# Attention feeding two expert stages: where the small constant of the softmax sums is added

## The chip, the cores and the metric

The kernel runs on one core of a Trainium2 chip. The metric is the device time of one execution in microseconds (us). TensorE is written PE in the rows (PEld is its weight load), VectorE is DVE, ScalarE is ACT, GpSimd is POOL and SyncE, which issues most of the transfers, is SP.

## The reference, cut to what matters

The program computes three things in a row, all in 32-bit floats: attention that keeps only the 32 largest scores of each row, a gated two-layer stage on all 2304 tokens, and a stage with eight experts of which each token uses its best two.

```python
# attention: 4 batches, 8 heads, 576 positions, width 64
scores = scale * np.matmul(q, k.transpose(0, 1, 3, 2))
kth = np.partition(scores, -32, axis=-1)[..., -32:-31]
scores = np.where(scores >= kth, scores, -1e9)
scores = scores - np.max(scores, axis=-1, keepdims=True)
attn = np.exp(scores)
attn = attn / (np.sum(attn, axis=-1, keepdims=True) + 1e-09)
x = np.matmul(attn, v)            # -> [2304, 512]
# gated stage
h = x @ w_in
x = (h * np.clip(h + 3.0, 0.0, 6.0) / 6.0) @ w_out
# eight experts, two for each token, weighted by a softmax over noisy logits
```

The change touches one thing: the `1e-09` in the divisor of the attention.

## The kernel before

The kernel has two parts. The first (`phase_a`, up to about 850 us) does the attention, and beside it the gated stage, and beside that, piece by piece, the logits and the routing of the experts. The second (`phase_b`) does the experts.

The attention works on 144 heads, called `i` below: 18 tiles of 128 rows with 8 heads each. A loop over steps `st` (line 584) runs them as a software pipeline. In one step, seven or more heads are in work, each at another stage: the transposed query of head `st` (`q_evac`), the scores of head `st-1` (`scores`, `s_evac`, which leave them in `ss`), the maxima of seven segments of head `st-1` (`seg`), the search in them for head `st-2` (`chain`, whose result is `a`), a mask `z` by `zmask` for head `st-2`, the product `y` of mask and scores by `ysum` and the exponential `e` by `expo` for head `st-3`, the search for the 32nd largest score in `y` (`ymax`, into `t`) and the masking of `e` with its row sum (`pmask`, into `sum`) for head `st-4`, then the transposes of `e` for head `st-5` (`ptrans`), and in every second step the product with V for a pair of heads (`av`). So a head pair takes two steps, and there are 72 pairs.

The row sums of a pair stand in one tile `sum` of 128 rows and 2 columns. In every second step three functions turn them into factors: `recip1` on GpSimd adds 1e-9 (line 413), `recip2` on VectorE takes the reciprocal (line 416), and `recip3` on GpSimd spreads it over 2x64 columns into `rb` (line 421), which TensorE transposes one step later.

Beside the attention, from step 25 on, each step does one unit `u` of the gated stage: 12 matmuls into `h` (`mm1`), a relu on ScalarE into `r` (`hrelu`), the gate on VectorE (`hgate`), a rounding on ScalarE into `g` (`hround`), the rest on GpSimd (`hlow`), and 6 matmuls into `xa` (`mm2`). There are 144 units, so they run on for about 15 steps after the attention.

Each engine runs its own instructions in order and waits only for semaphores. From step 22 on (`KEEP`) the order on the four computing engines is that in which the Python code issues the work; before that, and for what is filled in, a scheduler with a model of times decides it. Within a step the order on GpSimd is `hlow`, `ysum`, `recip1`, the small `nbias` (tile `a`), `recip3`, then the scaling of the attention's result (`xscale2` into `xs`, `xsplit` into `xT`), the splitting of queries and keys (`qsb`, `ksb`), and last what `fill` holds. On VectorE it is `ymax`, `recip2`, then `chain` and `seg` mixed, `hgate`, `zmask`, `pmask`, the last segments.

Three kinds of step carry more than this. Where a new batch begins, the keys of its eight heads are split and transposed too (`k_split`, `k_trans`). After each chunk of two tiles, TensorE does the logits of the experts (tiles `lt`, `lg`). After six tiles the routing of their tokens follows, with many small operations on GpSimd and VectorE and then twelve indirect transfers from GpSimd that scatter the token lists into `idw` (line 813), four in each of three consecutive head pairs.

The last two tiles are routed by VectorE while the expert stage has begun. Its matmuls are `hb` (first layer, line 935) and `ac` (second layer, line 959). The route's counting matmuls `po` (lines 784 to 789) stand among them in TensorE's order. Behind `po` come the last scatter into `idw`, the load of the token lists `id`, the gather of tokens `xg` (line 868), and the transposes `et` (line 899) of the next expert job.

Of the kernel before, what the change touches and what calls it, by code (L numbers as in the profile page):

```python
# [7 lines left out]
F32 = mybir.dt.float32  # L8
# [5 lines left out]
ALU = mybir.AluOpType  # L14
# [162 lines left out]
def phase_a(tc, pools, ident, q, k, v, w_in, w_out, X, worst, wscr, stream, begin, on_chunk=None, slots=NSLOT, pace=None):  # L177
    nc = Lanes(tc)
    wp, ap, mp, ps, dr = pools
    TS, TT, STT = nc.vector.tensor_scalar, nc.vector.tensor_tensor, nc.vector.scalar_tensor_tensor  # L180
# [57 lines left out]
    def k_load(i):  # L238
        dl, b, h = ksched[i]
        KR[i] = kr = ap.tile([128, 5, 64], F32, name=f"kr{i}", tag="kr", bufs=KRB)  # L240
        nc.sync.dma_start(kr[:, 0:4, :], k[b, h, 0:512, :].rearrange("(p j) d -> p j d", j=4))
        nc.sync.dma_start(kr[0:64, 4, :], k[b, h, 512:576, :])
# [53 lines left out]
    def q_load(t, g):  # L296
        QR[t, g] = qr = ap.tile([128, 4, 64], F32, name=f"qr{t}_{g}", tag="qr", bufs=QRB)
        for (b, row, n, s0) in pieces(t):
            nc.sync.dma_start(qr[row:row + n], q[b, 4 * g:4 * g + 4, s0:s0 + n, :].rearrange("h s d -> s h d"))
# [24 lines left out]
    def scores(i):  # L324
        t, h = divmod(i, 8)
        p = ps.tile([128, 2, 512], F32, name=f"s{i}", tag="s")
        qts = QT.pop(i)
        for half in range(2):
            n = 2 * len(qts)
            m = 0  # L330
            for qt, (b, _, _, _) in zip(qts, pieces(t)):
                for j in range(2):
                    nc.tensor.matmul(p[:, half, 0:288], qt[:, j, :],
                                     KT[b, h][:, half * 288:(half + 1) * 288],
                                     start=(m == 0), stop=(m == n - 1))
                    m += 1
        PSS[i] = p

    def s_evac(i):
        p = PSS.pop(i)  # L340
        ss = ap.tile([128, 576], F32, name=f"ss{i}", tag="ss", bufs=SSB)
        nc.scalar.copy(ss.rearrange("p (a n) -> p a n", a=2), p[:, :, 0:288])
        SS[i] = ss
        ST[i] = ap.tile([128, NSEG, 8], F32, name=f"seg{i}", tag="seg", bufs=SEGB)
# [23 lines left out]
    def expo(i):  # L368
        if i % 2 == 0:
            EP[i // 2] = ap.tile([128, 1152], F32, name=f"e{i}", tag="e", bufs=EB)  # L370
        e = EP[i // 2][:, 576 * (i % 2):576 * (i % 2) + 576]
        E[i] = e
        nc.scalar.activation(e, SS[i], AF.Exp, bias=A8[i][:, 24:25], scale=0.125)
# [7 lines left out]
    def ysum(i):  # L381

        Y[i] = y = ap.tile([128, 584], F32, name=f"y{i}", tag="y", bufs=YB)
        nc.gpsimd.tensor_tensor(y[:, 0:576], Z.pop(i), SS[i], op=ALU.mult)

        nc.scalar.activation(y[:, 576:584], rank, AF.Relu, bias=fillc, scale=low[:, i:i + 1])
# [17 lines left out]
    SUM = {}  # L404

    def pmask(i):
        if i % 2 == 0:
            SUM[i // 2] = ap.tile([128, 2], F32, name=f"sum{i}", tag="sum", bufs=3)
        STT(E[i], SS.pop(i), T8[i // 8][:, i % 8, 7:8], E[i], op0=ALU.is_ge, op1=ALU.mult,
            accum_out=SUM[i // 2][:, i % 2:i % 2 + 1])  # L410

    def recip1(p):
        nc.gpsimd.tensor_scalar(SUM[p], SUM[p], 1e-9, 1.0, op0=ALU.add, op1=ALU.mult)

    def recip2(p):
        nc.vector.reciprocal(SUM[p], SUM[p])

    def recip3(p):
        r = SUM.pop(p)
        rb = ap.tile([128, 2, 64], F32, name=f"rb{p}", tag="rb", bufs=2)  # L420
        nc.gpsimd.tensor_scalar(rb, r[:, :, None].to_broadcast([128, 2, 64]), 1.0, 1.0, op0=ALU.mult, op1=ALU.mult)
        RB[p] = rb
# [42 lines left out]
    def xscale(p):  # L465
        xs = ap.tile([128, 256], F32, name=f"xs{p}", tag="xs", bufs=XSB)
        copy('a', xs, AVP.pop(p)[:, 0:256])
        XR[p] = xs
# [23 lines left out]
    def w_fetch(u):  # L492
        c, fb = u
        if fb in stream:
            w = wp.tile([128, 2, 1024], F32R, name=f"ws{c}_{fb}", tag="ws", bufs=NSTR)
            nc.sync.dma_start(w.bitcast(F32), wscr[fb])
            W[u] = w
        else:
            W[u] = wres[fb]

    def mm1(u):
        c, fb = u
        n = 128 * len(chunks[c])
        w = W[u][:, :, 0:512].rearrange("p a (d f) -> p a d f", d=4)
        xt = XT[c]
        p = ps.tile([128, 512], F32, name=f"h{c}_{fb}", tag="h")
        m = 0
        for d in range(4):
            for a, b in ((0, 0), (0, 1), (1, 0)):
                o = nc.tensor.matmul(p[:, 0:n], w[:, a, d, :], xt[b][:, d, 0:n], start=(m == 0), stop=(m == 11))  # L510
                m += 1
        HP[u] = p
        lastmm[:] = [o]
# [14 lines left out]
    def hround(u):  # L528
        n = 128 * len(chunks[u[0]])
        g = mp.tile([128, 2, 256], F32R, name=f"g{u[0]}_{u[1]}", tag="g", bufs=GB)  # L530
        copy('g', g[:, 0, 0:n], R[u][:, 0:n])
        G[u] = g

    def hlow(u):
        n = 128 * len(chunks[u[0]])
        g = G[u]

        eng = nc.vector if ustep_of[u] > slots + OD else nc.gpsimd
        low = eng.tensor_tensor(g[:, 1, 0:n], R.pop(u)[:, 0:n], g.bitcast(F32)[:, 0, 0:n], op=ALU.subtract)
        if pace is not None:  # L540
            pace[:] = [low] if eng is nc.gpsimd else []
# [37 lines left out]
    ok = lambda i: 0 <= i < slots  # L579
# [4 lines left out]
    for st in range(-6, end):  # L584
        if st == -6: q_load(0, 0)
        if st == BEGIN: begin()
        if st == KEEP: nc.keep()
        if st % 4 == 0 and 0 < st // 4 + 1 < slots // 4: q_load(*divmod(st // 4 + 1, 2))
        for i, (dl, b, h) in enumerate(ksched):
            if max(dl - 4, min(i, 2) - 6) == st: k_load(i)  # L590
        for fb in wstep.get(st + 2, []): wk.load(fb)

        while fetched < len(units) and units[fetched][0] <= st + 3:
            w_fetch(units[fetched][1]); fetched += 1
        u, up = ustep.get(st), ustep.get(st - 1)
        s_, a, b, c, d, e, av_, x1, x2 = (st - x for x in (OS, OA, OB, OC, OD, OE, OV, OX, OY))
        ki = kdl.get(st)

        if up:
            hround(up)  # L600
            hlow(up)
        if ok(s_):
            scores(s_)
            s_evac(s_)
        if ok(c):
            ysum(c)
            expo(c)
        if ok(d - 1) and d % 2 == 0: recip1(d // 2 - 1)
        if u:
            mm1(u)  # L610
            hrelu(u)
        if ok(e):
            ptrans(e)
            ptevac(e)
        if ki is not None or ok(st):
            kq_trans(ki, st if ok(st) else None)
        if ok(st): q_evac(st)
        if ok(x1) and x1 % 2 == 0: xscale(x1 // 2)

        ch = chain(b) if ok(b) else []  # L620
        segs = [(a, j) for j in range(NSEG)] if ok(a) else []
        if ok(d): ymax(d)
        if ok(d - 1) and d % 2 == 0: recip2(d // 2 - 1)
        if ch:
            ch.pop(0)()
            nbias(b)
        while ch:
            if segs: seg(*segs.pop(0))
            ch.pop(0)()
        if segs: seg(*segs.pop(0))  # L630
        if u: hgate(u)
        if ok(b): zmask(b)
        if ok(d):
            pmask(d)
        while segs: seg(*segs.pop(0))

        if ok(d - 1) and d % 2 == 0: recip3(d // 2 - 1)
        if ok(x1) and x1 % 2 == 0: xscale2(x1 // 2)
        if up:
            mm2(up)  # L640
            if up[1] == NFB - 1: xout(up[0])
        if ki is not None:
            k_trans(ki)
            k_evac(ki)
        if ok(av_) and av_ % 2: av(av_ // 2)
        for i, (dl, b, h) in enumerate(ksched):
            if dl + VL == st: v_load(i)
        if ok(x2) and x2 % 2 == 0: xsplit(x2 // 2)
        if st % 4 == 2 and 0 <= st // 4 + 1 < slots // 4: q_split(*divmod(st // 4 + 1, 2))
        for i, (dl, b, h) in enumerate(ksched):  # L650
            if max(dl - 2, min(i, 2) - 5) == st: k_split(i)
        for fb in wstep.get(st, []): w_split(fb)
        for fb in wstep.get(st + 1, []): wk.convert(fb)
        room = NFILL if st < slots + OD else 3 * NFILL
        while fill and room > 0:
            room -= fill[0][0]
            fill.pop(0)[1]()
# [669 lines left out]
```

## Time and profile before

| | us |
|---|---|
| median of 3 runs | 1393.41 |
| lowest and highest of them | 1392.29, 1394.97 |
| the profiled execution's own time | 1381.3 |
| its span, first to last instruction | 1379.5 |
| mean granted TensorE clock, as a share of 2.4 GHz | 0.975 |

The rows come from one profiled execution. A row of the timeline gives the start, the duration, the engine, the operation, the tiles written and read, and in brackets the idle time of the engine before it with what ended it. The view of stretches gives, for a window in us, its length and then each engine's busy time with the number of instructions, then the granted TensorE clock, the share of busy transfer engines and GB/s. A TensorE that is busy is not at its peak: its matmuls overlap, and their ends are modelled.

### The profile page before, as it was taken

What the parts mean: (1) busy time and instruction counts of PE and PEld (TensorE: products, weight loads), DVE (VectorE), ACT (ScalarE), POOL (GpSimd) and SP (SyncE); (2) the same over time, 40 slices, a digit from 0 to 9 for tenths busy, and PEclk for the clock granted to TensorE, in tenths of its full rate; (3) what the DMA queues carried; (4) which work ended last, traced back from release to release, by engine and by line L of the source; (5) the groups of instructions that cost most, each with busy time, mean ns of one, the idle gap of its engine ahead of it and who ended that gap; (6) DMA issues with size and microseconds to landing.
All of it is one profiled execution on the core that took longest, in us unless ns stands there. A gap on an engine that the chain in (4) does not pass through costs nothing. (4 is left out here: it accounts for less than half of the span.)

```text
span 1379.5 us, 27084 instructions
## 1 busy us (share of the span) xinstructions
PE 1293.2 (94%) x9006; PEld 1121.2 (81%) x9006; DVE 948.3 (69%) x3560; ACT 770.2 (56%) x1709; POOL 829.9 (60%) x1159
## 2 busy tenths in 40 slices
PE   5878899999999989999999899899999999999996
PEld 3554689989888878898988688788988898898985
DVE  7999987899987978869989753446353545435241
ACT  6888777777778666777777554534322322222220
POOL 7666777677767786767687845133324547465451
PEclk9789999999999999999999999999999999999999
DMA  7776644545365353445544447846446556465431
GB/s 249 261 279 226 230 145 157 193 166 176 132 206 166 127 149 124 170 131 187 175 143 157 123 154 246 265 140 221 136 153 195 178 167 204 140 214 177 137 109 38
DMA packets 138100, 239.56 MB, mean 174 GB/s; under 512 B 39779, under 2 KB 93155, under 8 KB 123872
## 3 DMA queue, kind: packets, MB, share of 16 engines
q1 hardware_dynamic: 127600, 210.57, 46.1%
q0 software_dynamic: 10352, 27.18, 5.9%
q8 instruction: 73, 1.20, 0.4%
q14 instruction: 75, 0.61, 0.2%
HBM read 209.08 MB, written 31.64 MB: 174 GB/s over the span
## 5 line engine op out<-in xcount | busy, mean ns | idle before, releaser
L959 PE MATMUL ac<-w,hh 128*128 128x512 f32 x960 | 247.8, 400 | 1.6 <-ACT hh L941 1.5
L935 PE MATMUL hb<-xe,w 128*128 128x320 f32 (+2 forms) x1536 | 239.4, 311 | 1.0 <-DVE hh L942 0.5
L935 PEld LDWEIGHTS hb<-xe,w 128*128 128x128 f32 x1536 | 232.1, 189 | 10.0 <-issue 3.9
L87 DVE MAX8 seg<-ss 128x8 f32<-128x82 f32 (+1 forms) x1008 | 213.9, 231 | 4.1 <-ACT ss L87 3.7
L87 POOL TENSOR_TENSOR y<-z,ss 128x576 f32<-128x576 bf16 x144 | 205.3, 1426 | 11.7 <-DVE z L87 10.1
L941 ACT ACTIVATE hh<-hb 128x640 fp32r<-128x640 f32 (+2 forms) x72 | 46.6, 647 | 295.7 <-PE hb L935 295.7
L959 PEld LDWEIGHTS ac<-w,hh 128*128 128x128 f32 x960 | 172.8, 188 | 40.3 <-ACT hh L941 5.4
L942 DVE SCALAR_TENSOR_TENSOR hh<-hb,hh 128x640 fp32r<-128x640 f32 (+2 forms) x72 | 53.9, 749 | 213.2 <-ACT hh L941 213.2
L87 PE MATMUL h<-xT,ws 128*128 128x256 f32 x1188 | 159.1, 283 | 9.3 <-DVE r L87 7.9
L87 ACT COPY ss<-s 128x576 f32<-128x576 f32 x144 | 92.6, 643 | 134.6 <-DVE e L87 69.6
L87 PE MATMUL xa<-ws,g 128*128 128x512 f32 x594 | 163.9, 410 | 2.2 <-POOL g L87 0.9
L87 PEld LDWEIGHTS h<-xT,ws 128*128 128x128 f32 x1188 | 150.0, 190 | 12.8 <-DVE r L87 9.9
L921 POOL TENSOR_TENSOR w<-r,w 128x1024 fp32r<-128x1024 f32 x40 | 97.9, 2452 | 85.2 <-ACT w L919 73.4
L87 DVE SCALAR_TENSOR_TENSOR e<-ss,t,e 128x576 f32<-128x576 f32 x144 | 147.6, 1025 | 0.1
L87 POOL TENSOR_TENSOR g<-r,g 128x256 fp32r<-128x256 f32 x124 | 100.2, 808 | 39.8 <-issue 19.6
L87 PEld LDWEIGHTS xa<-ws,g 128*128 128x128 f32 x594 | 104.0, 190 | 23.6 <-POOL g L87 5.1
L87 DVE TENSOR_SCALAR_CACHE_REDUCE z<-ss,a 128x576 bf16<-128x576 f32 x144 | 115.8, 804 | 0.2
L87 ACT ACTIVATE e<-ss,a 128x576 f32<-128x576 f32 x144 | 110.6, 768 | 1.4 <-POOL a L87 1.4
L87 PE MATMUL s<-kt,qt 128*128 128x288 f32 x512 | 101.2, 321 | 7.8 <-ACT qt L87 6.8
L87 DVE MAX8 t<-y 128x8 f32<-128x584 f32 x144 | 107.8, 749 | 0.0
L975 POOL DMA_INDIRECT out_dram<-y,id x40 | 41.8, 1045 | 108.9 <-DVE y L974 86.7
L87 PE MATMUL pa<-ident,e 128*128 128x128 f32 x576 | 91.3, 283 | 15.4 <-DVE e L87 13.4
(427 smaller groups left out, 2617.2 us busy)
## 6 DMA issues: line engine op xcount, KB each, us to landing
ws<-wscr SPq DMA_DIRECT2D x99, 1024.0 KB, 4.8
r<-in_moe_w_dram SPq DMA_DIRECT2D x144, 256.0 KB, 3.1
wscr<-wsp SPq DMA_DIRECT2D x11, 1024.0 KB, 5.8
wraw<-in_moe_w_in_dram SPq DMA_DIRECT2D x16, 512.0 KB, 4.2
wraw<-in_moe_w_out_dram SPq DMA_DIRECT2D x16, 512.0 KB, 5.1
ck<-in_moe_w_in_dram SPq DMA_DIRECT2D x32, 256.0 KB, 3.4
ck<-in_moe_w_out_dram SPq DMA_DIRECT2D x32, 256.0 KB, 3.2
out_dram<-zero SPq DMA_DIRECT2D x18, 256.0 KB, 4.2
```

The lines of the kernel that those rows point to most:

```text
L87: o = f(*args, **kw)
L921: eng.tensor_tensor(w[:, 1], r, w.bitcast(F32)[:, 0], op=ALU.subtract)
L935: o = nc.tensor.matmul(p[:, half, 0:hn], w[:, a, d, :], XE[job][:, b, d, half * hn:(half + 1) * hn], start=(m == 0), stop=(m == 11))
L941: nc.scalar.activation(hv[:, 0], p[:, 0:nh, 0:hn], AF.Relu)
L942: LOW[:] = [STT(hv[:, 1], p[:, 0:nh, 0:hn], 0.0, h.bitcast(F32)[:, :, 0:n].rearrange("p a (b n) -> p a b n", b=nh)[:, 0], op0=ALU.max, op1 ...
L959: o = nc.tensor.matmul(ACC[job, j], h[:, a, j * 128:(j + 1) * 128], w[:, b, :], start=(x % NF2 == 0 and m == 0), stop=(x % NF2 == NF2 - 1 ...
L975: s = nc.gpsimd.indirect_dma_start(out=out, out_offset=bass.IndirectOffsetOnAxis(ap=t.bitcast(I32)[:, j, 1:2], axis=0), in_=y, in_offset=N ...
```

## The change

The addition of 1e-9 goes from GpSimd to VectorE. `recip1` and its call in the step are gone. `recip2` now has two instructions: a tensor_scalar with an accumulator output, which adds the constant to the two sums in place and writes the sum of the two results into a third column that nobody reads, and the reciprocal. The tile has a third column for it.

```diff
     def pmask(i):
         if i % 2 == 0:
-            SUM[i // 2] = ap.tile([128, 2], F32, name=f"sum{i}", tag="sum", bufs=3)
+            SUM[i // 2] = ap.tile([128, 3], F32, name=f"sum{i}", tag="sum", bufs=3)
...
-    def recip1(p):
-        nc.gpsimd.tensor_scalar(SUM[p], SUM[p], 1e-9, 1.0, op0=ALU.add, op1=ALU.mult)
-
     def recip2(p):
-        nc.vector.reciprocal(SUM[p], SUM[p])
+
+        TS(SUM[p][:, 0:2], SUM[p][:, 0:2], 1e-9, None, op0=ALU.add, op1=ALU.add, accum_out=SUM[p][:, 2:3])
+        nc.vector.reciprocal(SUM[p][:, 0:2], SUM[p][:, 0:2])
 
     def recip3(p):
-        r = SUM.pop(p)
+        r = SUM.pop(p)[:, 0:2]
...
-        if ok(d - 1) and d % 2 == 0: recip1(d // 2 - 1)
```

Lines below the edits stand two lower after it (935 becomes 933, 959 becomes 957).

VectorE's order at a head pair in the middle of the attention, before. The wait in brackets names the engine whose semaphore the instruction waits for; `t` is the result of `ymax`, `y` GpSimd's product, `ss` the scores.

```order
L87 SCALAR_TENSOR_TENSOR e_5563,sum_5695<-ss_5474,t_5177,e_5563 128x576
L87 MAX seg_5724<-ss_5722 128x8 x2
L87 MAX t_5852<-y_5725 128x8 [waits Pool_49]
L87 RECIPROCAL sum_5695<-sum_5695 128x2 [waits Pool_49]
L87 MAX a_5851<-seg_5724 128x8 [waits DVE_49]
L87 MAX seg_5812<-ss_5810 128x8 [waits Activation_49]
```

The same place after the change:

```order
L87 SCALAR_TENSOR_TENSOR e_5563,sum_5695<-ss_5474,t_5176,e_5563 128x576
L87 MAX seg_5724<-ss_5722 128x8 x2
L87 MAX t_5851<-y_5725 128x8 [waits Pool_49]
L87 TENSOR_SCALAR sum_5695<-sum_5695 128x2 [waits DVE_49]
L87 RECIPROCAL sum_5695<-sum_5695 128x2 [waits DVE_49]
L87 MAX a_5850<-seg_5724 128x8
```

The reciprocal no longer waits for GpSimd. It and the new instruction wait for VectorE's own semaphore instead.

The scheduler also places some other work anew: in the first 22 steps much of VectorE's order is changed, and later a few rows move. One such place lies at the start of the expert stage. TensorE's order there, before (`po` are the counting matmuls of the last routing, `hb` and `ac` the expert's two layers):

```order
L935 MATMUL hb_13958<-xe_13882,w_1_13892 128x384 x12
L959 MATMUL ac_0_13974<-w_0_13886,hh_13935 128x512
L959 MATMUL ac_1_13978<-w_0_13886,hh_13935 128x512
L959 MATMUL ac_2_13982<-w_0_13886,hh_13935 128x512
L784 LDWEIGHTS tri
L784 MATMUL po_13837<-oh_13774,tri 128x16
```

And after the change:

```order
L957 MATMUL ac_0_13974<-w_0_13886,hh_13935 128x512
L957 MATMUL ac_1_13978<-w_0_13886,hh_13935 128x512
L957 MATMUL ac_2_13982<-w_0_13886,hh_13935 128x512
L957 MATMUL ac_0_13974<-w_1_13892,hh_13971 128x512 x2
L957 MATMUL ac_1_13978<-w_1_13892,hh_13971 128x512 x2
L957 MATMUL ac_2_13982<-w_1_13892,hh_13971 128x512 x2
L933 MATMUL hb_13992<-xe_13882,w_2_13898 128x384 x12
L957 MATMUL ac_0_13974<-w_1_13892,hh_13971 128x512
L957 MATMUL ac_1_13978<-w_1_13892,hh_13971 128x512
L957 MATMUL ac_2_13982<-w_1_13892,hh_13971 128x512
L782 LDWEIGHTS tri
L782 MATMUL po_13837<-oh_13774,tri 128x16
```

The counting matmuls now stand behind 21 more matmuls: 6 of `ac`, 12 of `hb` and 3 of `ac`.

## Rows read from the trace of the kernel before

**Rows 1.** The page: span, then busy time, share and instructions of each engine.
```profile
span 1379.5 us, 27084 instructions
PE 1293.2 (94%) x9006; PEld 1121.2 (81%) x9006; DVE 948.3 (69%) x3560; ACT 770.2 (56%) x1709; POOL 829.9 (60%) x1159
```

**Rows 2.** Waits of VectorE, 0 to 814 us: total, times, longest.
```profile
DVE sum L87 <- POOL sum L87: 90.8, 62, 4.8
DVE seg L87 <- ACT ss L87: 3.7, 10, 0.6
```

**Rows 3.** Timeline, an ordinary head pair, 367 to 378 us.
```profile
367.94 0.17 DVE L87 RECIPROCAL sum<-sum 128x2 f32<-128x2 f32 x1 [0.48 <-POOL sum L87]
377.70 0.17 DVE L87 RECIPROCAL sum<-sum 128x2 f32<-128x2 f32 x1 [0.49 <-POOL sum L87]
```

**Rows 4.** Stretches: the start, where the first eight pairs run.
```profile
27.00:136.80 109.80, 84.17 (x431) 54.46 (x431) 108.65 (x395) 90.60 (x177) 73.54 (x90) 0.84 0.72 254
```

**Rows 5.** Stretches, 12 ordinary pairs: 269.3 to 337.7 and 638.0 to 687.1, sum.
```profile
sum 117.50, PE 117.50 PEld 105.28 DVE 109.16 ACT 87.90 POOL 83.92; mean PE 58.75 PEld 52.64 DVE 54.58 ACT 43.95 POOL 41.96
```

**Rows 6.** Stretches, the other 25 ordinary pairs in seven windows, sum.
```profile
sum 250.80, PE 244.81 PEld 219.45 DVE 223.18 ACT 174.49 POOL 173.76; mean PE 34.97 PEld 31.35 DVE 31.88 ACT 24.93 POOL 24.82
```

**Rows 7.** Stretches, 12 pairs with new keys, in three windows, sum.
```profile
sum 143.50, PE 140.65 PEld 126.20 DVE 106.17 ACT 115.84 POOL 101.23; mean PE 46.88 PEld 42.07 DVE 35.39 ACT 38.61 POOL 33.74
```

**Rows 8.** Stretches, six pairs with scatters, in two windows, and their sum.
```profile
488.40:527.20 38.80, 34.66 (x251) 30.12 (x249) 28.27 (x125) 24.50 (x62) 32.20 (x44) 0.91 0.46 134
749.90:787.90 38.00, 33.59 (x250) 29.14 (x248) 28.25 (x125) 24.01 (x61) 31.43 (x43) 0.96 0.44 130
sum 76.80, PE 68.24 PEld 59.27 DVE 56.51 ACT 48.51 POOL 63.63; mean PE 34.12 PEld 29.63 DVE 28.26 ACT 24.26 POOL 31.82
```

**Rows 9.** Timeline, a pair with scatters, 499 to 516 us.
```profile
501.89 0.17 DVE L87 RECIPROCAL sum<-sum 128x2 f32<-128x2 f32 x1 [4.79 <-POOL sum L87]
...
503.87 2.93 PE L87 MATMUL h<-xT,ws 128*128 128x256 f32 x12 [3.34 <-DVE r L87]
```

**Rows 10.** Stretches, nine pairs heavy on VectorE (136.8 to 181.6, 434.8 to 478.8), sum.
```profile
sum 88.80, PE 79.21 PEld 66.58 DVE 81.95 ACT 62.90 POOL 65.58; mean PE 39.60 PEld 33.29 DVE 40.98 ACT 31.45 POOL 32.79
```

**Rows 11.** Groups by line: busy us, mean ns of one, idle before it.
```profile
L87 DVE TENSOR_SCALAR_CACHE_REDUCE z<-ss,a 128x576 bf16<-128x576 f32 x144 | 115.8, 804 | 0.2
L87 DVE RECIPROCAL sum<-sum 128x2 f32<-128x2 f32 x72 | 11.8, 165 | 91.8 <-POOL sum L87 91.7
L87 DVE DVE_READ_ACCUMULATOR z<-ss,a 128x1 f32 x144 | 11.8, 82 | 0.0
```

**Rows 12.** Timeline of VectorE, two dependent small operations at 848.8 us.
```profile
848.79 0.19 DVE L771 TENSOR_REDUCE rs<-rt 128x4 f32<-128x32 f32 x1
849.01 0.19 DVE L772 TENSOR_TENSOR rt<-rt,rs 128x32 f32<-128x32 f32 x1
```

**Rows 13.** One tile, e on VectorE: duration minimum, median and maximum in ns.
```profile
L87 DVE SCALAR_TENSOR_TENSOR e<-ss,t,e x144: 789/862/2444, 27.1 to 812.5; 128x576 f32<-128x576 f32 x144
```

**Rows 14.** The chain that ended last, 886 to 925 us: start, us, what.
```profile
906.36 5.75 DMA idw<-pl,ix
...
914.57 5.03 DMA xg<-X,id
919.60 0.04 issue
919.64 0.66 PE et L899 x4
```

**Rows 15.** Timeline of TensorE, 862 to 925 us.
```profile
899.59 0.18 PE L784 MATMUL po<-oh,tri 128*128 128x16 bf16 x1
...
903.27 2.46 PE L959 MATMUL ac<-w,hh 128*128 128x512 f32 x9
...
919.64 0.66 PE L899 MATMUL et<-ident,xg 128*128 128x128 f32 x4 [2.41 <-DMA xg<-X,id]
```

## The prediction

> **What bounds the kernel now.** I read the page first. Over the whole span TensorE is busy 94% and VectorE 69% [rows 1], but that averages the attention with the expert stage, so I went on by stretches and looked at the waits of the engine that is changed.
>
> In the attention VectorE waits for almost nothing except GpSimd's addition: 90.8 us in 62 waits, the longest 4.8 us, against 3.7 us for the next kind [rows 2]. The reason is the order on GpSimd. The addition stands behind `ysum`, the product of 1.3 us or more, of the same step. VectorE needs that product only one step later, but through `recip1` it waits for it at once.
>
> Whether those 91 us set the time is another question, and the stretches answer it by kind of head pair. In each I ask what TensorE does while VectorE waits.
> - The first eight pairs, 27 to 136.8 us: VectorE is busy 108.65 of 109.80 us [rows 4]. It is the bound, and it does not wait for GpSimd's addition.
> - 12 ordinary pairs: TensorE is busy all 117.50 us, VectorE idle 8.3 us [rows 5]. A pair takes 9.8 us. The usual one has a wait of only 0.48 or 0.49 us [rows 3]. TensorE is the bound, as far as the rows tell.
> - 25 more ordinary pairs, some with logits: TensorE idle 6.0 of 250.80 us, VectorE idle 27.6 [rows 6]. Nearly the same.
> - 12 pairs with new keys: VectorE idle 37.3 us, but TensorE only 2.85 [rows 7]. The large waits here lie beside extra work of TensorE.
> - Six pairs with scatters: TensorE idle 8.6 us of 76.80, and its granted clock is 0.91 and 0.96 of 2.4 GHz [rows 8]. Here a wait of 4.79 us in front of the reciprocal makes the gate late, and TensorE then waits 3.34 us for the gate [rows 9].
> - Nine pairs heavy on VectorE (routing, and steps that lack units): TensorE idle 9.6 us, VectorE 6.85 [rows 10].
>
> So most of VectorE's wait lies beside a busy TensorE. Only the time in which TensorE is idle or slowed can come back.
>
> **The change, part by part.** It removes 72 additions and the waits for them, 91.7 us in front of the reciprocals over the whole kernel [rows 11].
>
> It adds two instructions to each pair on VectorE, the addition and the read of its accumulator, and a wait of the reciprocal for the addition's result. The trace has no such pair with two columns. From above it costs what the mask `z` with 576 columns does, 0.80 + 0.08 = 0.89 us; from below two reads of the accumulator, 0.16 us [rows 11]. The nearest row is a pair of dependent small operations, 0.22 us from start to start [rows 12]. With 0.08 for the read I take 0.30 us, 72 x 0.30 = 22 us for the whole kernel. In 62 pairs it stands where a wait for GpSimd goes [rows 2], mostly of 0.48 us or more, so it costs nothing there beyond making the gain smaller. In the first eight there is hardly such a wait and VectorE is the bound: 8 x 0.30 = 2.4 us, at least 1.3 and at most 7.
>
> The gain, by kind:
> - Scatter pairs: TensorE can win its 8.6 us idle and what the low clock took. 0.09 x 38.8 + 0.04 x 38.0 = 5.0 us at most. Together 13.6 us. GpSimd is late next: it is busy 63.63 of the 76.80 us [rows 8], which allows 13.2. It still waits now and then for ScalarE and VectorE, so I take 9.
> - Nine VectorE-heavy pairs: 6.85 us idle less 9 x 0.30 = 2.7 gives 4.
> - Pairs with new keys: TensorE's idle 2.85 us, so 3. VectorE then waits for ScalarE's relu in front of the gate.
> - 37 ordinary pairs: half of TensorE's 6.0 us, so 3.
> Sum of the attention: 19 us. Its bounds: nothing, and VectorE's whole wait less its new work, 91.7 - 22 = 70 us.
>
> GpSimd loses 72 small operations and spreads the sums right behind `nbias` as before. The spread needs the reciprocal, which now comes earlier. `sum` has three buffers as before, and the third column is read by nobody.
>
> **The scheduler's moves.** In the first 22 steps VectorE's order changes, but VectorE is busy 99% there [rows 4], so an order alone can win little. I count zero, with 4 us to either side.
> The move at the start of the expert stage is worth more. The last route's counting matmuls `po` began at 899.59 us. Now 6 `ac`, 12 `hb` and 3 `ac` stand ahead of them. In the trace that stretch ends behind the third of the nine `ac` that begin at 903.27 and take 2.46 with their overlap, at about 904.0 [rows 15]. So `po` comes 4.4 us later. What follows is the chain that ended last: scatter, token list, gather, and then the transposes `et` at 919.64 [rows 14], for which TensorE already waits 2.41 us [rows 15]. TensorE's order behind it is the same, so all of it is late: +4.4 us. Bounds: zero, if the scatter is held by something else, and 7, if TensorE's clock falls in the longer wait.
>
> **The sum.** -19 + 2.4 + 4.4 = -12 us against the profiled execution's own 1381.3 us: 1369. The median of the runs shown, 1393.41, is 0.9% above that execution, so I scale: 1393.41 x 1369.3 / 1381.3 = 1381.
>
> **Where the Trainium skill bears on it.** TensorE's busy time is 100% in the ordinary pairs, its weight loads 105.28 of 117.50 us, 90% [rows 5]. [...]
> The masking of `e` takes 789 ns at least, 862 in the median and up to 2444 [rows 13]. "GPSIMD Engine Reference", section "Key points", says that GpSimd shares its paths to SBUF with VectorE and that instructions with two SBUF inputs contend; the masking has two. By that rule time won could be lost again beside GpSimd, the second rival. The spread of the durations agrees with it.
>
> **The rivals.**
> 1. TensorE has room in the ordinary pairs, and VectorE's idle time is the limit there too. For it: VectorE is busy 93% in rows 5. Against it: TensorE's rows there leave no gap. VectorE is idle 8.3 + 27.6 = 35.9 us in the 37 pairs [rows 5, 6]; less 37 x 0.30 = 11 that is 25 instead of the 3 above, 22 us more: -34, or 1359.
> 2. VectorE and GpSimd collide. Without the wait GpSimd's products overlap more of VectorE's masking. If each of 144 maskings went 0.07 us above its present median [rows 13], VectorE would lose 10 us in all, and the whole would come to about -2: 1391, no change. For it: that spread. Against it: TensorE, not VectorE, is the bound in most pairs.
> 3. The other side: the delay of `po` decides. It costs 4.4 us and, if TensorE's clock falls in the longer wait, 7. If TensorE's order and ScalarE hold the attention so firmly that it wins under 5 us, the start's 2.4 us and this make it slower. With 2 us won and 7 lost: +7, 1401. For it: TensorE is idle under 3% of the time in the ordinary pairs and in those with new keys [rows 5 to 7], and the delay lies on the last chain [rows 14]. Against it: in the scatter pairs TensorE is seen to wait for the gate [rows 9].
> That the change does not do what it says I rule out by the order: the reciprocal no longer waits for GpSimd.
>
> **How the numbers follow.** The forecast, 1366 to 1390, has a chance of 0.66, rival 1 0.12, rival 2 0.12, rival 3 0.10. What a measurement of this kernel tells from no change is 0.2%, 2.8 us. Nearly all of the forecast and rival 1 and a sixth of rival 2 are faster by more: 0.79. Same: 0.11, slower: 0.10. The range goes from 1357, with rival 1 in it, to 1395, with rival 2 and the mild cases of rival 3; left out are a gain near the bound of 70 us and rival 3 at its full price.
>
> **What would show it.** Right: VectorE has no wait for GpSimd in front of the reciprocal; addition, read and reciprocal together take about 0.4 us; the ordinary pairs keep 9.6 to 9.8 us; the six scatter pairs come down from 76.8 to about 68 us with the clock near 1.00; the gap in front of `et` grows from 2.4 to about 6.8 us; VectorE's new waits are for ScalarE (`seg`, `r`). Wrong: ordinary pairs near 9.2 us (rival 1), maskings longer than 0.93 us in the median (rival 2), or an attention that ends less than 5 us earlier (rival 3). The weakest steps are TensorE's limit in the pairs with new keys and the nine VectorE-heavy pairs.

## The result, and the profile after

The changed kernel takes 1378.23 us (median of 4 runs, 1377.34 to 1383.01) against 1394.19 for the kernel before (median of 4): ratio 0.9892, 95% interval 0.9864 to 0.992. That is 16.0 us, where 12 were predicted (1381 of 1393). The two profiled spans are only 2.3 us apart, 1377.2 and 1379.5 [rows 1], because the profiled execution of the kernel before was 13 us shorter than its timed runs. Which chip these runs used is not on record; on two later chips, where both kernels ran side by side, the change won 8 and 9 us (below). So each mark is read in two or three profiles.

The page of the changed kernel, the span and the busy time of each engine:

```profile
span 1377.2 us, 27159 instructions
PE 1288.4 (94%) x9006; PEld 1116.6 (81%) x9006; DVE 948.5 (69%) x3704; ACT 769.2 (56%) x1709; POOL 812.8 (59%) x1087
```

VectorE has 144 instructions more and the same busy time as in [rows 1], GpSimd 72 fewer and 17 us less. The waits of VectorE up to 800 us (total, times, longest), and its groups on `sum` (busy us, mean ns of one, idle before):

```profile
DVE seg L87 <- ACT ss L87: 60.3, 64, 2.6
DVE r L87 <- ACT r L87: 6.9, 9, 1.4
...
DVE t L87 <- POOL y L87: 4.5, 4, 1.1
```

```profile
L87 DVE RECIPROCAL sum<-sum 128x2 f32<-128x2 f32 x72 | 11.8, 164 | 2.1
L87 DVE TENSOR_SCALAR_CACHE_REDUCE sum<-sum 128x2 f32<-128x2 f32 x72 | 9.6, 134 | 0.0
L87 DVE DVE_READ_ACCUMULATOR sum<-sum 128x1 f32 x72 | 5.7, 80 | 0.0
```

The wait of 90.8 us for GpSimd's sum [rows 2] is gone. Two thirds of it have come back one instruction later, as waits for ScalarE's `ss`, which themselves stand behind TensorE's scores. The timeline of VectorE in an ordinary pair shows the exchange:

```profile
366.75 0.75 DVE L87 MAX8 t<-y 128x8 f32<-128x584 f32 x1
367.42 0.13 DVE L87 TENSOR_SCALAR_CACHE_REDUCE sum<-sum 128x2 f32<-128x2 f32 x1
367.48 0.08 DVE L87 DVE_READ_ACCUMULATOR sum<-sum 128x1 f32 x1
367.59 0.17 DVE L87 RECIPROCAL sum<-sum 128x2 f32<-128x2 f32 x1
367.67 0.20 DVE L87 MAX8 a<-seg 128x8 f32<-128x56 f32 x1
368.16 0.25 DVE L87 MAX8 seg<-ss 128x8 f32<-128x82 f32 x1 [0.29 <-ACT ss L87]
```

From the addition's start to the reciprocal's it is 0.17 us here, 0.177 in the median of 72; the three together take 0.34, where about 0.4 was predicted.

**Where the time went.** The 72 reciprocals of the row sums mark the head pairs in every profile. The distance from one to another, in us, in two profiles of the kernel before and three of the changed one:

| from reciprocal to reciprocal | before | changed |
|---|---|---|
| 1 to 9, the start | 103.5, 106.2 | 104.7, 104.5, 107.3 |
| 9 to 13, VectorE-heavy | 37.0, 38.1 | 35.6, 36.5, 35.8 |
| 13 to 21, new keys and behind | 87.7, 87.7 | 86.9, 87.3, 86.9 |
| 21 to 33, ordinary | 118.2, 118.2 | 118.1, 118.1, 118.1 |
| 33 to 41, new keys, then routing | 91.4, 91.3 | 91.0, 91.0, 91.1 |
| 42 to 49, scatters and behind | 79.9, 79.9 | 73.4, 73.3, 73.4 |
| 49 to 55, new keys and behind | 69.7, 69.7 | 68.9, 68.9, 68.9 |
| 55 to 66, ordinary | 111.8, 111.8 | 111.9, 111.8, 111.9 |
| 66 to 72, scatters and behind | 64.3, 64.3 | 58.4, 58.3, 58.7 |
| 9 to 72, all of these | 669.6, 670.7 | 653.3, 654.4, 653.9 |

Outside the start the distances repeat within some tenths, on different chips. The attention gains 16 us, and 12 of them lie in the two stretches with scatters. TensorE's waits there, before (reciprocals 42 to 49, then 66 to 72) and after, show what went. `h` is the first matmul of the gated stage and `r` VectorE's gate:

```profile
PE h L87 <- DVE r L87: 5.7, 3, 3.3
PE h L87 <- DVE r L87: 5.9, 3, 2.7
```

```profile
PE xa L87 <- POOL g L87: 1.9, 2, 1.0
PE xa L87 <- POOL g L87: 2.5, 3, 1.0
```

The wait for the gate, 11.6 us, is gone, and what is left is mostly a wait for `g` from GpSimd. GpSimd's additions themselves took only 1.34 and 1.15 us in these two stretches before, so the work taken off GpSimd can't be the 12 us.

The view of stretches (length, busy time of PE, PEld, DVE, ACT and POOL with their instructions, granted clock, DMA share, GB/s) shows for the kernel before the scatter pairs with the pair behind them:

```profile
488.40:537.20 48.80, 42.70 (x309) 37.41 (x308) 37.79 (x166) 28.92 (x72) 39.54 (x55) 0.90 0.49 140
749.90:797.90 48.00, 41.31 (x316) 35.95 (x315) 37.76 (x166) 29.31 (x73) 38.11 (x53) 0.96 0.49 144
```

And for the changed kernel, first 12 ordinary pairs, then the same scatter pairs with the pair behind them:

```profile
268.60:386.70 118.10, 118.01 (x968) 106.18 (x967) 108.84 (x522) 86.02 (x215) 80.22 (x115) 1.00 0.48 159
486.90:530.60 43.70, 40.63 (x328) 35.41 (x326) 39.04 (x174) 30.36 (x75) 36.80 (x51) 1.00 0.61 164
741.10:783.70 42.60, 40.08 (x323) 34.82 (x322) 37.66 (x173) 29.80 (x74) 35.76 (x50) 1.00 0.57 163
```

The clock, 0.90 and 0.96 before, is 1.00 in both. TensorE is still idle for 5.6 us of them. In the ordinary pairs it stays busy all the time, and nothing is gained.

Behind the attention a part is given back. TensorE's row at the transposes of the next job, with the gap in front of it:

```profile
902.55 0.86 PE L957 MATMUL ac<-w,hh 128*128 128x512 f32 x3
910.05 1.12 PE L897 MATMUL et<-ident,xg 128*128 128x128 f32 x4 [6.63 <-DMA xg<-X,id]
910.82 2.91 PE L957 MATMUL ac<-w,hh 128*128 128x512 f32 x6
```

The gap was 2.41 us [rows 15]. In it the clock falls to 0.5, at 906.7 us, and stays there for 6.8 us: `et` takes 1.12 us instead of 0.66, and six `ac` take 2.91 where nine took 2.46. In the two later profiles of the changed kernel the gap was 4.95 and 6.51 us. From the last reciprocal to the 97th `hb`, behind all this, it is 123.1, 126.1 and 125.5 us, against 116.3 and 120.5 before.

### The profile page after: what moved, and what is told of

It is laid out like the page before. It is cut to its first block, busy times and chain, and to the rows that moved or that the text cites. A ratio compares the mean times of both kernels' runs of the same rounds, so it can differ in the third digit from the quotient of the medians.

```text
span 1377.2 us, 27159 instructions
## 1 busy us (share of the span) xinstructions
PE 1288.4 (94%) x9006; PEld 1116.6 (81%) x9006; DVE 948.5 (69%) x3704; ACT 769.2 (56%) x1709; POOL 812.8 (59%) x1087
## 4 chain that ended last, share of the span: by engine, by line
PE 64%; DVE 6%; issue 5%; ACT 4%; POOL 3%; DMA 1%; another core or an unknown queue 1%; POOLq 0%; ACTq 0%; SPq 0%
PE ac L957 15%; PE hb L933 15%; PE xa L87 10%; PE h L87 9%; PE av L87 5%; PE s L87 4%; PE pa L87 2%; DVE seg L87 2%; POOL idw L811 1%; DVE e L87 1%; PE et L897 1%; DVE z L87 1%; ACT ss L87 1%; DVE t L87 1%; PE lg L727 1%
## 5 line engine op out<-in xcount | busy, mean ns | idle before, releaser
L87 POOL TENSOR_TENSOR y<-z,ss 128x576 f32<-128x576 bf16 x144 | 201.2, 1397 | 14.7 <-DVE z L87 12.9
L87 DVE SCALAR_TENSOR_TENSOR e<-ss,t,e 128x576 f32<-128x576 f32 x144 | 143.6, 997 | 0.1
L87 POOL TENSOR_TENSOR xs<-xs 128x128 f32<-128x128 f32 x72 | 51.7, 718 | 119.4 <-ACT xs L87 119.3
L87 POOL TENSOR_TENSOR g<-r,g 128x256 fp32r<-128x256 f32 x124 | 96.4, 778 | 24.2 <-issue 9.2
```

Source lines behind the costliest of these rows:

```text
L87: o = f(*args, **kw)
```

## The experiments

My theory: VectorE stands behind GpSimd's `ysum` for nothing, but only where TensorE has room is the wait worth anything, and the late `po` gives some back. The rivals: VectorE is the limit nearly everywhere (rival 1 of the prediction), the new order of the start or of the scheduler makes the gain, or the form of the addition matters.

The runs used three more chips, on which the kernel before took 1398.12 us (the two kernels again, GpSimd ahead of `ysum`, `po` held ahead for the first time), 1384.95 us (the reciprocal later, four additions, no addition and the plain form for the first time) and 1385.00 us (the changed kernel for the third time, and every second measurement). So every time is compared by its ratio to the kernel before on its chip, and an expectation in us that was reckoned for another chip can't be held against the time; the marks in the traces can.

**The two kernels again, on another chip.** No edit.

> The kernel before, unchanged, for a second profile. Its first profiled execution took 1381.3 us, its timed runs 1394. Theory A: that execution was an unusually short one, and the extra 13 us lie in the attention (more stretches at half clock, or longer pairs): a second profile ends near 1394 and its last reciprocal of a row sum comes near 825 instead of 814 us. Theory B: they lie in the expert stage, behind 880 us: the last reciprocal stays at 814 and the time behind it grows by 13. If the profile again takes 1381, the profiled executions of this kernel are 13 us shorter than its timed ones for a reason that no row shows.

> The changed kernel, unchanged, for a second profile. Theory: 1378 us again; the attention ends (last reciprocal of a row sum) at 799 us, 13 to 15 before that of the kernel before. The new waits of TensorE behind the 13th et (for hh from ScalarE, some 6 us from there to the end in the first profile) come back if they follow from the change; if they were an accident of one execution they are gone and the profile ends near 1372.

Measured: 1399.33 us, and 1391.83 for the changed kernel, ratio to the kernel before 0.9941 (0.9908 to 0.9973). In the profile of the kernel before the last reciprocal came at 818.4 (3 of the 4 us from the start), and from the 97th `hb` to the end it took 464.6 us instead of 449.0: theory B for most of it. The changed kernel's last reciprocal came at 800.3, and TensorE's waits for `hh` came back, 8.9 us. The kernel before had 9.2 us of them here, so they belong to neither kernel alone. ScalarE pauses; its rows in the changed kernel:

```profile
1038.59 0.57 ACT L902 CAST xe<-et 128x512 fp32r<-128x512 f32 x1
1048.17 0.70 ACT L939 ACTIVATE hh<-hb 128x640 fp32r<-128x640 f32 x1 [9.01 <-issue]
```

Its input was complete 4.3 us before. In a third profile of the changed kernel (below) the same instruction started at once:

```profile
1041.76 0.58 ACT L902 CAST xe<-et 128x512 fp32r<-128x512 f32 x1
1047.09 0.71 ACT L939 ACTIVATE hh<-hb 128x640 fp32r<-128x640 f32 x1 [4.75 <-PE hb L933]
```

**GpSimd adds, ahead of `ysum`.** From the kernel before:

```diff
+        if ok(d - 1) and d % 2 == 0: recip1(d // 2 - 1)
         if ok(c):
             ysum(c)
             expo(c)
-        if ok(d - 1) and d % 2 == 0: recip1(d // 2 - 1)
```

> The kernel before with one line moved: GpSimd still adds the constant, but ahead of ysum instead of behind it. VectorE gets no new work, and the start and TensorE's order there stay as before; po comes late as in the changed kernel. My theory (the gain is the removed wait behind ysum, whoever adds): the wait in front of the reciprocal nearly goes, the last reciprocal comes 14 to 17 us earlier, the time is 1374 to 1381 us. Rival 1 (the gain comes from the new order of the first 22 steps or from taking work off GpSimd): no gain, 1392 to 1398. Rival 2 (GpSimd now waits at that addition for VectorE's masking, and ysum behind it is late): half the gain, 1383 to 1390, with new waits of GpSimd for sum.

Measured: 1393.81 us, ratio 0.9977 (0.9945 to 1.0009). From the 9th to the 72nd reciprocal it took 662.0 us, 8 less than before: half the gain. The time, with `po` late, is only 4.3 us under the 1398.12 of this chip. By the marks that is rival 2, with the waits that it named (VectorE, then GpSimd, 150 to 800 us):

```profile
DVE sum L87 <- POOL sum L87: 32.1, 23, 3.5
DVE sum L87 <- issue: 12.1, 4, 3.9
```

```profile
POOL sum L87 <- DVE e L87: 16.9, 22, 2.0
```

VectorE's and TensorE's order in the start is the old one here, so the new order of the start is not the source of this half.

**The reciprocal issued later.** From the kernel before; the call of `recip2` moves from in front of `chain` to behind it:

```diff
         if ok(d): ymax(d)
-        if ok(d - 1) and d % 2 == 0: recip2(d // 2 - 1)
...
+        if ok(d - 1) and d % 2 == 0: recip2(d // 2 - 1)
         if segs: seg(*segs.pop(0))
         if u: hgate(u)
```

> The kernel before with the reciprocal issued later in its step on VectorE, behind the search of chain and six of the segments, about 2 us on; GpSimd still adds, in its old place behind ysum. VectorE gets no new work and should find the sum ready. po comes late as in the changed kernel. My theory (the wait of VectorE is all that the change removes): the waits for sum fall from 91 us to under 20, the last reciprocal comes at 797 to 802 us instead of 814 to 818, 1386 to 1392 us on this chip. Rival (taking the addition off GpSimd matters as well, or the spread rb, which now comes later, holds up xs): the last reciprocal no earlier than 806.

Measured: 1383.48 us, ratio 0.9991 (0.9978 to 1.0003), and 663.0 us from the 9th to the 72nd reciprocal, 7 less than before. The last reciprocal at 808.1: the rival. VectorE's wait fell to 20.1 us, but GpSimd now waits for the reciprocal (waits of VectorE, then of GpSimd, 150 to 800 us):

```profile
DVE seg L87 <- ACT ss L87: 67.9, 68, 3.0
DVE sum L87 <- POOL sum L87: 20.1, 12, 5.7
```

```profile
POOL rb L87 <- DVE sum L87: 42.4, 40, 1.9
```

At the first scatters (reciprocals 42 to 49) it took 81.1 us, no less than before. There GpSimd itself is late, and only an addition that isn't behind its work helps: 73.4 in the changed kernel, 75.8 with GpSimd's addition ahead of `ysum`. My theory was too simple: it is not only VectorE's wait that costs, but the chain from GpSimd to VectorE and back to GpSimd. Each of the two runs eases one end of it and has about half the gain.

**Four additions instead of one, and none.** From the changed kernel:

```diff
-        TS(SUM[p][:, 0:2], SUM[p][:, 0:2], 1e-9, None, op0=ALU.add, op1=ALU.add, accum_out=SUM[p][:, 2:3])
+        (four times this line, with 5e-10; or no such line)
```

> The changed kernel with the addition and the read of its accumulator four times in a row instead of once (each adds 5e-10); po late as in the changed kernel. One addition with its read took 0.23 us from its start to that of the reciprocal, so VectorE gets 3 x 0.23 = 0.7 us more in each of 72 pairs, 50 us in all. My theory (outside the first eight pairs VectorE has room, since it now waits 61 us for ScalarE's scores): 5.5 us in the start, and of the other 44 us about a third, 12 to 25 us later in the last reciprocal. Rival 1 of the prediction (VectorE is the limit in the ordinary pairs): all of it, 45 to 50 us later. If VectorE has room everywhere but in the start: 5 us.

> The changed kernel without the addition: 1e-9 is left out. VectorE has 72 x 0.23 = 17 us less to do; po stands ahead of the ac of w_1 again, as in the kernel before, so the fair comparison is the changed kernel with po held first (1383 us on this chip). My theory (the added work costs something in the start and in the pairs heavy on VectorE alone): the start 1.8 us earlier, the last reciprocal 2 to 5 us earlier, 1378 to 1382 us. Rival 1 (VectorE is the limit nearly everywhere): the last reciprocal 12 to 17 us earlier, 1366 to 1371 us.

> The changed kernel without the addition (1e-9 left out), po ahead, beside the changed kernel with po held ahead. Theory (the added work on VectorE is nearly all hidden outside the start): within 2 us of that kernel, and 0 to 2 us under it. Rival 1 of the prediction (VectorE is the limit): 10 to 17 us under it.

Measured: with four 1388.21 us, ratio 1.0027 (1.0015 to 1.0039), which is slower than the kernel before. The last reciprocal came at 814.9, 12 to 15 us later than in the changed kernel, as the theory has it. From the 9th to the 72nd it took 665.2 us, 11 more than the changed kernel, where the new work is 38 us (0.77 us from the first addition to the reciprocal instead of 0.18, 63 times). The 12 ordinary pairs that took 118.10 us took 119.40:

```profile
275.00:394.40 119.40, 118.90 (x973) 106.59 (x973) 115.21 (x594) 87.32 (x217) 80.94 (x115) 1.00 0.47 161
```

VectorE's busy time grew by 6.4 us there and the stretch by 1.3, so VectorE isn't the limit; TensorE, busy 118.90 us, is the one left. In the 11 others (55th to 66th reciprocal) it was 115.5 us, 3.6 more for 6.5 of new work: there the room for more is small. Between the 9th and the 13th it was 38.8 us, 3 more for 2.4 of new work: VectorE is the limit there. The 5.5 us expected in the start did not appear there: the first reciprocal came 2 us later, at 43.5, and from it to the 9th took 106.1 us, inside the changed kernel's 104.5 to 107.3.

Without the addition: 1369.43 us, ratio 0.9882 (0.9864 to 0.99), and in the second measurement 1370.17, ratio 0.9899 (0.9883 to 0.9916), beside 1372.78 for the changed kernel with `po` ahead. From the 9th to the 72nd reciprocal it took 652.6 and 652.0 us, 1 to 2 less than with the addition. The last reciprocal, at 798.9 and 799.2, is less than 4 us earlier, not 12 to 17. Its start has an order of its own, and the stretch from the 42nd to the 49th is the same 73.3 and 73.4 us, so the order of the start doesn't make the gain. The first time lies in the bracket of rival 1, but that was reckoned for the chip where the kernel before took 1398. In the second measurement the difference of the medians is 2.6 us, a little over the 2 expected. So the 12.7 us that it adds on VectorE (72 x 0.177 from its start to the reciprocal's; the 0.23 of the expectations was too much) cost 1 to 2 in the path. Rival 1 is out for work of this size. In the reference the largest term of each row is exp(0) = 1, so the sum is at least 1, and 1e-9 lies far under the spacing of 32-bit floats there: leaving it out is, by the medians, the fastest version that was tried.

**`po` held ahead.** From the changed kernel, an order without a wait, as in the kernel before:

```diff
+            PO[:] = [o]                                 # o: the last counting matmul
...
+                    if g == 2: after(tc, o, PO[0])      # hb of w_2
...
+                    if g == 1: after(tc, o, PO[0])      # ac of w_1
```

> The changed kernel with the counting matmuls po held ahead of the ac of w_1 and the hb of w_2, as in the kernel before; everything else stands as in the changed kernel. My theory (the move of po gives back 4.4 us at the start of the expert stage): the gap in front of the 13th et falls from 6.6 to about 2.4 us, no stretch at half clock follows it, 1370 to 1375 us. Rival (the move is hidden, since the gather or ScalarE decides there): the same 1378 within 2 us.

> The changed kernel with po held ahead, as before, now compared with the changed kernel where it may be measured more closely. Theory (late po gives back 4.4 us and more, with half clock behind the gap): 4 to 8 us under the changed kernel. Rival (the 9 us seen so far were the other chip's pauses of ScalarE): within 2 us of it.

> The changed kernel, unchanged, as the reference for the three others on this chip. The last reciprocal at 799 to 801 us as in both profiles so far. From the 84th hb on, the time to the end was 455 us where ScalarE never paused and up to 16 us more where it did; if the pauses belong to the chip and not to the kernel, all four kernels here have them or none.

Measured: 1382.98 us, ratio 0.9899 (0.9869 to 0.993), where the changed kernel had 0.9941; then 1372.78, ratio 0.991 (0.9893 to 0.9928), beside 1375.57 for the changed kernel, 0.9936 (0.9921 to 0.9951). So 3 to 9 us by the medians, though the intervals overlap. The 2.8 us of the second measurement lie between the theory there (4 to 8) and its rival (within 2): part of the 9 us seen first were pauses of ScalarE, as the profiles say (from the 84th `hb` to the end 469.2 us, in the changed kernel there 475.3). By the medians it is under both kernels in both measurements. TensorE's rows in its second profile:

```profile
894.36 0.17 PE L785 MATMUL po<-oh,tri 128*128 128x16 bf16 x1 [2.44 <-DVE oh L777]
...
913.39 0.66 PE L901 MATMUL et<-ident,xg 128*128 128x128 f32 x4 [1.57 <-DMA xg<-X,id]
```

The gap in front of `et` is 1.57 us (none in the first profile), and the clock does not fall behind it. But TensorE now waits 2.44 us in front of `po` for VectorE's `oh`, which is last there: the routing allows little more. In this profile `po` came so late, 94.6 us behind the last reciprocal, that the way to the 97th `hb` took 124.5 us, as in the changed kernel; in the first it took 118.9.

**The plain form of the addition.** From the changed kernel; the order on every engine is the same:

```diff
-        TS(SUM[p][:, 0:2], SUM[p][:, 0:2], 1e-9, None, op0=ALU.add, op1=ALU.add, accum_out=SUM[p][:, 2:3])
+        TS(SUM[p][:, 0:2], SUM[p][:, 0:2], 1e-9, 1.0, op0=ALU.add, op1=ALU.mult)
```

> The changed kernel with the plain form of the addition, which has no accumulator to read; every engine's order stays that of the changed kernel. The read takes 0.08 us, 72 of them 5.8 us. My theory: 1 to 2 us earlier at the last reciprocal, no difference that the times can tell from the changed kernel's 1392 on this chip. If the plain form is slower by itself (another mode of the instruction), the pair from addition to reciprocal takes more than 0.23 us and the last reciprocal is not earlier.

> The changed kernel with the plain form of the addition, on the same chip as the changed kernel. In its first profile 72 plain additions took 33 us, 0.28 us in the median and up to 1.72, most of them ending 23 to 33 ns after a running product of GpSimd; with accumulator an addition took 0.13 us, 0.16 at most. Theory (the plain form is held until GpSimd's instruction ends, the form with accumulator is not): the last reciprocal 3 to 4 us later than in the changed kernel, the time 2 to 4 us longer. Rival (the 33 us lie beside a busy TensorE, and the later reciprocal was chance): within 1 us.

Measured: 1379.21 us, ratio 0.9954 (0.9938 to 0.9971); then 1380.04, ratio 0.9966 (0.9951 to 0.9981), against 1375.57 for the changed kernel on the same chip. The plain form is the slower one, by 4.5 us in the medians (the ends of the intervals meet) and with the last reciprocal 3.1 us later, though it has one instruction fewer. The tile on VectorE (duration minimum, median, maximum in ns), the plain form and then the changed kernel on that chip:

```profile
L87 DVE TENSOR_SCALAR sum<-sum x72: 142/280/1711, 41.3 to 805.1; 128x2 f32<-128x2 f32 x72
```

```profile
L87 DVE TENSOR_SCALAR_CACHE_REDUCE sum<-sum x72: 124/133/155, 41.1 to 802.4; 128x2 f32<-128x2 f32 x72
```

The timeline says why. First the plain form, beside GpSimd's product, then the form with accumulator at the same place:

```profile
370.99 1.81 POOL L87 TENSOR_TENSOR y<-z,ss 128x576 f32<-128x576 bf16 x1
372.55 0.28 DVE L87 TENSOR_SCALAR sum<-sum 128x2 f32<-128x2 f32 x1
372.86 0.17 DVE L87 RECIPROCAL sum<-sum 128x2 f32<-128x2 f32 x1
```

```profile
368.75 1.81 POOL L87 TENSOR_TENSOR y<-z,ss 128x576 f32<-128x576 bf16 x1
370.31 0.13 DVE L87 TENSOR_SCALAR_CACHE_REDUCE sum<-sum 128x2 f32<-128x2 f32 x1
370.37 0.08 DVE L87 DVE_READ_ACCUMULATOR sum<-sum 128x1 f32 x1
370.48 0.17 DVE L87 RECIPROCAL sum<-sum 128x2 f32<-128x2 f32 x1
```

The plain addition ends at 372.83, 0.03 us after GpSimd's product (372.80). The other ends at 370.44, while the product runs on to 370.56. In the second profile 56 of the 72 plain additions took over 0.2 us, and 54 of these ended 20 to 35 ns after a running product of GpSimd. The Trainium skill, "SBUF — State Buffer", section "Who interferes with whom", says the same: a tensor_scalar may need the port that VectorE shares with GpSimd and is then held until GpSimd's instruction ends, but not in the form that also writes out its accumulator. The trace agrees: of the changed kernel's additions on this chip, 64 began beside a running instruction of GpSimd, and none took over 0.155 us.

## Why the prediction was right

The time, the sign and most of the mechanism came as predicted; the size of single terms did not, and the number owes something to luck.

- **VectorE's wait for GpSimd goes.** So it was, and the waits for `ss` and `r` came as said.
- **Cost of the added pair, 0.30 us.** It is 0.18 from start to start. In the start +2.4 us was taken; the five profiles with the new order and accumulator (three of the changed kernel, two with `po` ahead) average 105.3 us from the 1st to the 9th reciprocal, and the four with the old order 104.0. That is +1.3, with a spread of 3 to 4 in each, so it isn't settled. Without the addition the start took 105.4 and 106.0 us and with four 106.1, each in an order of its own: no run shows the term.
- **Scatter pairs, 9 of at most 13.6 us.** 12.4 us, near the bound (6.5 and 5.9). The clock came back to 1.00, and what TensorE still waits for is mostly GpSimd, as said. The four and three pairs behind them are included, since work also moved from one pair into the next: the six pairs alone took 60.0 us (30.2 and 29.8), where about 68 was the sign, but the pairs right behind them took 6.3 us more.
- **VectorE-heavy pairs, 4 us; new keys, 3; ordinary, 3.** Here the terms were too large, 10 us together and 3.8 in the trace: 1.6 between the 9th and the 13th reciprocal, 1.7 in the three stretches with new keys and the second routing, 0.5 between the 41st and 42nd, and nothing in 23 ordinary pairs. The step that failed is to count the idle time there, TensorE's or in the nine pairs VectorE's, as room for the reciprocal: with its wait gone, most of that time did not come back. The prediction had named two of these as its weakest steps. The errors cancel: 16 us in all instead of 19. That part is luck.
- **Ordinary pairs keep 9.6 to 9.8 us.** Single ones went to 9.1 and others to 11.1, but 12 of them took 118.1 as before. A single pair near 9.2 was given as a sign for rival 1; read over the stretch it is none.
- **The late `po`, +4.4 us, at most 7.** The gap grew from 2.4 to 6.6 us, as said. The way from the last reciprocal to the 97th `hb` became 6.5 us longer by the means of the five profiles above. Over all 14 profiles it is 124.4 us in the eight with `po` late (121.4 to 126.2) and 120.1 in the six with it ahead (116.3 to 124.5): 4.3 us, near the forecast, though the two groups overlap. Of these, 1.9 us lie between `et` and the 97th `hb`, where the clock is at half behind the longer gap. Holding `po` ahead gave 3 to 9 us of time back. The 7 was given without a working, and no run settles it.
- **Rival 2, collisions.** The masking's median is 816 ns, not over 930 and even under the 862 of [rows 13]:

```profile
L87 DVE SCALAR_TENSOR_TENSOR e<-ss,t,e x144: 803/816/3348, 27.1 to 798.4; 128x576 f32<-128x576 f32 x144
```

  The longest grew, but the mean fell from 1025 to 997 ns. Out.
- **Rival 3, under 5 us in the attention.** The last reciprocal came at 799.4 to 802.6 us instead of 814.2 and 818.4. Out.
- **The sum.** +1.3 - 16.2 + 4.3 = -10.6 us, where -12 was forecast. The two later chips with both kernels show 8.2 us (0.9941 of 1398.12, as a difference of the ratio from 1; 6.3 by the medians) and 9.4 (1385.0 less 1375.57). The first measurement showed 16.0. Pauses of ScalarE like those above may explain the rest, if the timed runs of the kernel before had more of them, or two chips may have been compared; the timed runs of the kernel before have no trace, so it stays open.

## What to carry to other kernels

A wait is worth what the bounding engine does beside it: 91 us of waits gave 16, and 12 of them where TensorE stood still and its clock had fallen. When a small operation moves from GpSimd to VectorE, look at the form of the instruction as well as at its engine. Compare stretches between marks that both traces have, not spans, and not single pairs.

## What the runs showed of the hardware that was not expected

- The plain addition of two columns took up to 1.72 us beside GpSimd's products, the form with accumulator at most 0.16.
- ScalarE's pauses come back at the same places of the expert stage (in front of the relu behind the 264th, 480th, 672nd and 864th `hb`, now and then the 1056th or 1080th). They last 1 to 5 us each. All four profiles of one chip have them, at three or all of the first four places, and none of the others save the first of the changed kernel. They make up to 16 us of an execution. What ScalarE waits for there, no row shows.
